# A gated recurrence with a maxout network behind it: the first part reordered around products of constants, block loads split, a third output buffer

## The chip, the cores and the metric

The kernel runs on one core of a Trainium2 chip. The metric is the device time of one execution in microseconds, from launch to end; several runs of the same kernel give a median and a spread. All tensors lie in the chip's memory when the program starts, and the outputs lie there when it ends.

## The reference

The work has two stages. The first is a gated recurrence over 768 time steps, for 4 batches and 8 heads of dimension 48:

```python
f = 1.0 / (1.0 + np.exp(-f_logit))
for t in range(S):                                        # S = 768
    state = f[:, :, t, :, None] * state + einsum('bhd,bhe->bhde', k[:, :, t], v[:, :, t])
    y[:, :, t] = einsum('bhd,bhde->bhe', q[:, :, t], state)
x = y.transpose(0, 2, 1, 3).reshape(B * S, H * D)         # 3072 x 384
h = maximum(maximum(x @ w1, x @ w2), x @ w3)              # 384 -> 768
out = h @ w_out                                           # 768 -> 384
```

The second is a network on its 3072 rows: three products from 384 to 768 columns, their element-wise maximum, and a product back to 384. The four weight matrices arrive as 64-bit floats, everything else as 32-bit floats.

## The kernel before

**Units.** The recurrence is cut into 24 units. A unit holds 64 time steps of 2 batches, so 128 rows. Four units, 512 rows, make a group, and each group goes through the network as one "FFN": FFN 0 for units 0 to 3, up to FFN 5 for units 20 to 23. Within a unit the recurrence is done in its chunked form: running products of the gates from both ends of the chunk, a masked 64x64 product of queries and keys per head and batch, and a state of 48x48 per head that is carried from unit to unit of the same two batches.

**Stages of a unit**, each a function, with the engines in it:

- `load` and `load_v`: the loads of f, k, q and of v, all issued by SyncE (SP). The first eight units load rows, two transfers per tensor (L158). Later units load two at a time as 32x32 blocks, 8 transfers per tensor and so 24 for two units (L173), issued in the pass of each even unit. v always comes by rows into four buffers.
- `sigmoids`: TensorE (PE) transposes f, ScalarE (ACT) takes the sigmoid (L251). For blocks, ACT takes the sigmoid, and VectorE (DVE) does the transposes in `after` and `before` (L238).
- `after`: a DVE scan of the gates (`r`, L273), the reciprocal, and `kh` from k. `before`: the second scan (`prod`, L287) and `qh` from q. The products that make `kh` and `qh` are on DVE for the first eight units and on GpSimd (POOL) later (L280, L291); for these later units q is first turned by DVE into `qt`.
- `carry`: POOL multiplies the old state with the unit's gate product.
- `keys`: PE transposes `kh` (L306), ACT copies the result to `ks` (L308).
- `pairs`: 32 small matrix passes of `kh` with `qh` into `a` (L319), then the mask product `at` on DVE (L322).
- `values`: passes of `at` with v (L333) and of `ks` with v (L342) into `y`, then DVE adds the carried state (L350).
- `finish`: passes of the state with `qh` into `y` (L363), then ACT copies `y` to `heads` (L369).
- `pack`: transfers that move `heads` to `xT`, the layout that the network reads (L380), ten for a whole group. They go out on SP alone, or on SP and ACT by turns.

**The network.** `ffn(g, xT)` is a Python generator. It has 18 input steps, 6 column blocks times w1, w2, w3, each of three 128x512 products (L392). ACT copies the first of three to `top` (L396), DVE takes the maxima of the other two with it, `top` and then `hm` (L398). Four output steps follow, each of six 128x384 products (L411), ACT's copy to `o` (L414) and two output transfers (L418). `fill(n)` takes n steps from the FFNs that are pending, so the order of the program places pieces of one group's network between the stages of the next group's units. PE runs a full-precision 32-bit product as two passes; the records of the trace count passes.

**The weights.** They are brought to 32 bits on the chip in 24 pieces, 18 of the input matrices and 6 of `w_out`. `load_weights` loads a piece into one of 12 `raw` buffers (L199). `round_begin` takes the upper and the lower words: ACT (L211), two short DVE operations (L212, L213), ACT (L216), and a POOL addition (L217). `round_end` has the last DVE operation (L225), which writes `w_in` or `w_out`. Pieces 0 to 2 are done in the first part of the program. The rest is done inside the steps of FFN 0, each `round_begin` one piece ahead of its `round_end`.

**Buffers.** PSUM holds two buffers of the FFN's products `p`, which the transposes of k and q of the first four units use too, two for transposes, one for `a`, one for `y`. Other tiles have two buffers unless said otherwise. The two sets of buffers for f, k, q change from rows to blocks at unit 8; `pad_blocks` then sets six stripes of them, with six POOL memsets each, after units 4 and 6 (L143).

**What sets the order.** The program is written out by hand: each engine runs its instructions in the order in which the Python code issues them, SP and ACT their transfers likewise, and the stages wait for each other through semaphores. A transfer's completion is counted on one of eight semaphores that SP and ACT share, and a transfer waits for the earlier one that used its semaphore. After all else, the kernel looks whether a gate product came out too small: DVE reduces `ends` to `least` (L539), PE sums it over the partitions (L542), the result goes to `low`, every engine reads it (L732), and a second way of doing the whole work is skipped by a branch (L733).

## Time and profile before

| what | value |
|---|---|
| three timed runs | 503.88, 501.72, 504.91 us; median 503.88 |
| the profiled execution: its time | 504.31 us |
| its span, first to last instruction | 502.6 us |
| mean granted TensorE clock | 0.966 |
| PE busy | 467.9 us (93%) |
| DVE busy | 217.2 us (43%) |
| ACT busy | 108.7 us (22%) |
| POOL busy | 98.7 us (20%) |
| chain that ended last | PE 80%, DVE 6%, DMA 4%, SP's queue 4% |

The profile divides the span into 40 slices of 12.6 us; a digit is the busy share in tenths, and the row PEclk has the clock that the throttle granted to PE, also in tenths. A row of the order of time has the start, the duration, the engine, the line, the operation with its output and inputs, and the count of records in the group; in brackets stands the idle time ahead of it and what released it. A row of the stretches has the stretch (from:to in us), its length, then busy time and count of PE, of PE's weight loads, of DVE, ACT and POOL, and in its last three columns the granted clock, the DMA share and the GB/s. A row of a line's transfers to landing has the least, the median and the largest time from issue to landing, of the transfers of one tile in a stretch. "SPq" and "ACTq" are the queues of transfer issues on SP and ACT. The page's row of a line has its busy time and the mean of one in ns.

### The profile page before, as it was taken

The numbers are of one execution on the slowest core, as the hardware profiler recorded it, in microseconds if no ns is written. First come the engines' busy times: TensorE is split into PE (matmuls) and PEld (weight loads), VectorE is DVE, ScalarE is ACT, GpSimd is POOL, SyncE is SP. The second block draws the span as 40 slices with busy tenths as digits, with TensorE's granted clock in tenths as the row PEclk, the third lists the DMA queues.
The fourth block names the chain that finished last, engine by engine and source line by source line (L and its number), as shares of the span: only waits on it lengthen the run. The fifth ranks groups of instructions, "written<-read, shape, count | busy, mean of one in ns | idle before, by whom it ended". The sixth has DMA issues, their size and how long they took to land.

```text
span 502.6 us, 9969 instructions
## 1 busy us (share of the span) xinstructions
PE 467.9 (93%) x4067; PEld 250.9 (50%) x4067; DVE 217.2 (43%) x346; ACT 108.7 (22%) x227; POOL 98.7 (20%) x132
## 2 busy tenths in 40 slices
PE   5755999996989999999999999999999999999994
PEld 4642555543635455645545654545644545544452
DVE  7852787787225435135535226533325620012100
ACT  2340445540212211202220211220220111100000
POOL 2111356564021212021112022112112200000000
PEclk9875999998999999999999999999999999999998
DMA  9995996720156612266602276402460011200011
GB/s 129 199 179 157 268 243 143 93 59 1 40 87 109 88 27 65 46 79 110 85 2 63 56 88 109 66 16 57 78 105 18 1 36 37 55 0 0 1 28 42
DMA packets 170007, 38.51 MB, mean 77 GB/s; under 512 B 154976, under 2 KB 168800, under 8 KB 169952
## 3 DMA queue, kind: packets, MB, share of 16 engines
q1 hardware_dynamic: 166208, 36.50, 41.5%
q10 hardware_dynamic: 3744, 1.28, 1.3%
q8 instruction: 34, 0.56, 0.5%
q14 instruction: 21, 0.17, 0.1%
HBM read 28.31 MB, written 4.72 MB: 66 GB/s over the span
## 4 chain that ended last, share of the span: by engine, by line
PE 80%; DVE 6%; DMA 4%; SPq 4%; ACT 1%; issue 1%; POOL 1%; ACTq 0%; DVEq 0%; POOLq 0%
PE p L392 53%; PE p L411 17%; SPq L158 3%; PE y L363 2%; PE y L333 2%; DMA xT<-heads 2%; PE a L319 2%; PE tr L306 2%; PE y L342 1%; DMA v_ld<-in_v_dram 1%; POOL top_bits L217 1%; PE tr L234 1%; DVE top_bits L213 1%; DMA k_ld<-in_k_dram 1%; DVE top_bits L212 1%
## 5 line engine op out<-in xcount | busy, mean ns | idle before, releaser
L392 PE MATMUL p<-xT,w_in 128*128 128x512 f32 x648 | 291.9, 602 | 7.3 <-DMA xT<-heads 5.1
L392 PEld LDWEIGHTS p<-xT,w_in 128*128 128x128 f32 x648 | 120.5, 191 | 147.0 <-issue 134.1
L411 PE MATMUL p<-w_out,hm 128*128 128x384 f32 x288 | 98.8, 501 | 4.3 <-DVE w_out L225 4.3
L411 PEld LDWEIGHTS p<-w_out,hm 128*128 128x128 f32 x288 | 55.5, 195 | 44.7 <-DVE w_out L225 5.6
L398 DVE TENSOR_TENSOR top<-p,top 128x512 f32<-128x512 f32 x36 | 24.8, 690 | 106.3 <-PE p L392 106.3
L396 ACT COPY top<-p 128x512 f32<-128x512 f32 x36 | 21.1, 586 | 191.5 <-PE p L392 191.5
L279 POOL COPY ends<-r 128x8 f32<-128x8 f32 x24 | 4.6, 193 | 194.2 <-DVE r L273 194.2
L398 DVE TENSOR_TENSOR hm<-p,top 128x512 f32<-128x512 f32 x36 | 24.6, 684 | 38.2 <-PE p L392 38.2
L322 DVE TENSOR_TENSOR at<-a,mask 128x512 f32<-128x512 f32 x24 | 16.5, 689 | 52.8 <-PE a L319 52.8
L217 POOL TENSOR_TENSOR top_bits<-top_bits,rest_bits 128x384 uint32<-128x384 uint32 x24 | 27.2, 1133 | 50.3 <-DVE top_bits L213 27.9
L414 ACT COPY o<-p 128x384 f32<-128x384 f32 x24 | 11.4, 477 | 107.8 <-PE p L411 99.0
L287 DVE TENSOR_TENSOR_SCAN prod<-gate,from_inv 128x520 f32<-128x520 f32 x24 | 32.4, 1349 | 0.0
L273 DVE TENSOR_TENSOR_SCAN r<-gate,from_one 128x520 f32<-128x520 f32 x24 | 30.9, 1288 | 2.9 <-issue 2.2
L369 ACT COPY heads<-y 64x256 f32<-64x256 f32 (+1 forms) x72 | 26.6, 369 | 14.3 <-PE y L363 13.3
L291 POOL TENSOR_TENSOR qh<-qt,prod 128x512 f32<-128x512 f32 x16 | 18.8, 1178 | 41.7 <-DVE qt L238 41.7
L333 PEld LDWEIGHTS y<-at,v_ld 64*64 64x64 f32 x768 | 13.9, 136 | 20.9 <-issue 16.7
L333 PE MATMUL y<-at,v_ld 64*64 64x64 f32 x768 | 17.3, 227 | 5.7 <-ACT rest_bits L216 2.7
L308 ACT COPY ks<-tr 128x512 f32<-128x512 f32 x22 | 12.9, 586 | 41.2 <-PE tr L306 40.9
L280 POOL TENSOR_TENSOR kh<-kt,r 128x512 f32<-128x512 f32 x16 | 19.0, 1186 | 14.2 <-DVE kt L238 14.2
L297 POOL TENSOR_TENSOR state<-st,ends 128x384 f32<-128x384 f32 x22 | 21.1, 958 | 0.2
L238 DVE STREAM_TRANSPOSE gate<-sig 128x512 f32<-128x512 f32 x16 | 11.3, 708 | 21.2 <-ACT sig L254 21.2
L319 PE MATMUL a<-qh,kh 48*64 48x64 f32 x768 | 16.5, 225 | 0.5 <-DVE qh L291 0.5
(64 smaller groups left out, 269.9 us busy)
## 6 DMA issues: line engine op xcount, KB each, us to landing
raw<-in_moe_w_dram SPq DMA_DIRECT2D x18, 384.0 KB, 5.1
v_ld<-in_v_dram SPq DMA_DIRECT2D x48, 96.0 KB, 3.3
out_dram<-o SPq DMA_DIRECT2D x48, 96.0 KB, 2.2
raw<-in_moe_w_out_dram SPq DMA_DIRECT2D x6, 384.0 KB, 4.1
xT<-heads SPq DMA_DIRECT2D x30, 72.0 KB, 2.1
f_ld<-in_f_logit_dram SPq DMA_DIRECT2D x32, 64.0 KB, 2.9
k_ld<-in_k_dram SPq DMA_DIRECT2D x32, 64.0 KB, 2.8
q_ld<-in_q_dram SPq DMA_DIRECT2D x32, 64.0 KB, 2.8
```

Source lines behind the costliest of these rows:

```text
L217: nc.gpsimd.tensor_tensor(top, top, rest, op=ALU.add)
L273: nc.vector.tensor_tensor_scan(r[:, 0:LEN][:, ::-1], flat(gate)[:, ::-1], flat(from_one)[:, ::-1], 1.0, op0=ALU.mult, op1=ALU.max)
L280: (nc.vector if u < BY_ROWS else nc.gpsimd).tensor_tensor(kh.rearrange("p h a t -> p a h t"), kt, by_batch(r[:, 1:LEN + 1].rearrange("p (x ...
L287: nc.vector.tensor_tensor_scan(flat(prod), flat(gate_tiles[u % 2]), flat(from_inv[u % 2]), 1.0, op0=ALU.mult, op1=ALU.max)
L297: nc.gpsimd.tensor_tensor(t, states[u % 2], ends[:, u, :].unsqueeze(2).to_broadcast([128, 2 * HP, D]), op=ALU.mult)
L319: nc.tensor.matmul(p[t, par, hp * C:(hp + 1) * C], lhsT=kh[r, hp, a, :], rhs=qh[r, a, hp, :], start=True, stop=True)
L333: nc.tensor.matmul(y[o:o + DP, a, hp * C:(hp + 1) * C], lhsT=v_ld[s, 2 * hp + par, :], rhs=d["at"][s, par, hp, :], start=(hp == 0), stop=F ...
L369: nc.scalar.copy(heads[o, :, t0 + a * C:t0 + (a + 1) * C], y[i, a, 0:HP * C].rearrange("p (h t) -> p h t", h=HP))
L392: nc.tensor.matmul(p, lhsT=w_in[i][:, kt, j * 128:(j + 1) * 128], rhs=xT[:, kt, :], start=(kt == 0), stop=(kt == NK - 1))
L396: nc.scalar.copy(top, p)
L398: nc.vector.tensor_tensor(hm[:, j, :] if i == 2 else top, p, top, op=ALU.max)
L411: nc.tensor.matmul(p[:, 0:DM], lhsT=hm[:, j, i * UT:(i + 1) * UT], rhs=w_out[:, j, :], start=(j == 0), stop=(j == NJ - 1))
```

## The change

It has seven parts.

1. **Rounding in three parts.** `round_begin` keeps the two ACT operations; the two DVE operations and the POOL addition become `round_middle`. The ACT operations of pieces 0 and 1 stand ahead of `values(2)`; within FFN 0 a piece is begun two ahead of its `round_end` instead of one.
2. **Order of the first loads and of the pack.** f(3) goes ahead of v(1), v(2) ahead of the first three weight pieces. Of unit 4 only f and k are loaded ahead of the pack; q and v are issued behind it.
3. **Products of constants.** `busy(n)` issues n products of the identity with `from_one`, 128x256 each, into a buffer `p` that nothing reads: one each after `pairs(1)`, `pairs(2)` and `pairs(3)`, and 14 behind `finish(3)` and the pack.
4. **Pads.** `pad_blocks` becomes a generator; each step of FFN 0, input or output, takes one memset of it.
5. **Output buffers.** `o` has three buffers instead of two.
6. **Block loads and unit 8.** At an odd unit u, the blocks of f for units u+3 and u+4 are loaded (for u of 5, 9, 13 and 17 those of all three tensors); for u of 7, 11, 15 and 19 k and q follow in the next unit's pass, k ahead of `values`, q behind the next `fill`. At unit 8 the fill ahead of `keys` is left out.
7. **The look at the gate products** stands behind eight fill steps after the last pack, ahead of the other steps of the last FFN, instead of at the end.

```diff
             def pad_blocks(i):
                 for nm, pad in PADS.items():
                     for p0 in (32, 96):
-                        nc.gpsimd.memset(blocks[nm][i][p0:p0 + 32, :, :, D - 32:], pad)
+                        yield nc.gpsimd.memset(blocks[nm][i][p0:p0 + 32, :, :, D - 32:], pad)
...
+            def words(n):
+                w = raw[n].rearrange("p (c two) -> p c two", two=2)
+                return w[:, :, 0], w[:, :, 1]
+
             def round_begin(n):
                 if n in raw:
-                    words = raw[n].rearrange("p (c two) -> p c two", two=2)
-                    lo, hi = words[:, :, 0], words[:, :, 1]
+                    lo, hi = words(n)
                     top = work.tile([128, PIECE], U32, name="top_bits", bufs=4)
                     nc.scalar.activation(top.bitcast(FP32), hi.bitcast(FP32), AF.Abs)
+                    rest = work.tile([128, PIECE], U32, name="rest_bits", bufs=3)
+                    nc.scalar.activation(rest, lo, AF.Copy, scale=2.0 ** -29)
+                    halfway[n] = (top, rest)
+
+            def round_middle(n):
+                if n in raw:
+                    top, rest = halfway[n]
                     nc.vector.tensor_scalar(top.bitcast(FP32), top.bitcast(FP32), HI_MIN, None, op0=ALU.max)
                     nc.vector.tensor_scalar(top, top, 3, 0x3FFFFFF8, op0=ALU.logical_shift_left, op1=ALU.bitwise_and)
-                    rest = work.tile([128, PIECE], U32, name="rest_bits", bufs=3)
-                    nc.scalar.activation(rest, lo, AF.Copy, scale=2.0 ** -29)
                     nc.gpsimd.tensor_tensor(top, top, rest, op=ALU.add)
-                    halfway[n] = (top, hi)
...
                                 round_end(r)
-                                if r + 1 < len(pieces):
-                                    round_begin(r + 1)
+                                if r + 2 < len(pieces):
+                                    round_begin(r + 2)
+                                    round_middle(r + 2)
                             load_weights(2, r + 1)
+                            next(pads, None)
...
-                    o = work.tile([UT, DM], FP32, name="o")
+                    if g == 0:
+                        next(pads, None)
+                    o = work.tile([UT, DM], FP32, name="o", bufs=3)
...
+            def busy(n):
+                p = ps_f.tile([128, TOK], FP32, name="p")
+                for _ in range(n):
+                    nc.tensor.matmul(p[:, 0:256], lhsT=ident, rhs=from_one.rearrange("p x t -> p (x t)")[:, 0:256],
+                                     start=True, stop=True)
+
+            pads = iter(())
...
                 load(2)
+                load(3, one, "f")
                 load_v(1)
-                load(3)
+                load(3, one, "kq")
+                load_v(2)
                 load_weights(3)
-                load_v(2)
                 load_v(3)
...
                     pairs(u + 1)
+                    busy(1)
                     finish(u)
                     before(u + 2)
...
+                for n in range(2):
+                    round_begin(n)
                 values(2)
+                for n in range(2):
+                    round_middle(n)
                 keys(3)
                 finish(2)
                 load_weights(3)
-                load(GRP)
-                load_v(GRP)
-                round_begin(0)
+                load(GRP, one, "fk")
                 pairs(3)
-                round_begin(1)
+                busy(1)
                 round_begin(2)
+                round_middle(2)
                 values(3)
-                for n in range(3):
-                    round_end(n)
-                round_begin(3)
+                round_end(0)
                 nc.tensor.transpose(ps_tr.tile([128, 128], FP32, name="tr"), ident, ident)
                 finish(3)
+                round_end(1)
+                round_end(2)
                 pack(0, GRP - 1, xT, both)
+                for n in range(3, 5):
+                    round_begin(n)
+                    round_middle(n)
+                busy(14)
+                load(GRP, one, "q")
+                load_v(GRP)
                 load_weights(3)
...
-                    fill(2 if u % 2 and u > 2 * GRP else 1)
+                    fill(0 if u == 2 * GRP else 2 if u % 2 and u > 2 * GRP else 1)
...
-                    if u + 2 < NU and (u % 2 == 0 or u + 2 < BY_ROWS):
+                    if u + 2 < BY_ROWS:
                         load(u + 2)
+                    if BY_ROWS <= u + 3 < NU and u % 2:
+                        load(u + 3, one, "fkq" if u % GRP == 1 else "f")
...
                     fill(1)
+                    if BY_ROWS <= u + 2 < NU and u % GRP == 0:
+                        load(u + 2, one, "k")
                     values(u)
                     if n < NU:
                         before(n)
                         carry(n)
                         if n in (5, 7):
-                            pad_blocks(n // 2 % 2)
+                            pads = pad_blocks(n // 2 % 2)
                     fill(1)
+                    if BY_ROWS <= u + 2 < NU and u % GRP == 0:
+                        load(u + 2, one, "q")
...
                 pending.append(ffn(NU // GRP - 1, xT))
+                fill(8)
+
+                least = work.tile([128, 1], FP32, name="least")
+                nc.vector.tensor_reduce(out=least, in_=ends.rearrange("p u a -> p (u a)"), op=ALU.min, axis=AX.X)
+                nc.vector.tensor_scalar(least, least, P_MIN, None, op0=ALU.is_lt)
+                n_low = ps_tr.tile([1, 1], FP32, name="tr")
+                nc.tensor.matmul(n_low, lhsT=least, rhs=ones, start=True, stop=True)
+                nc.vector.tensor_copy(low, n_low)
                 fill(99)
```

The lines removed at the end are the same five that are added above it, without the fill.

How the instructions move shows at three places. In the orders, a number behind a name is its buffer: v_ld_128 to v_ld_131 are the four buffers of v (units 0 to 3, then 4 to 7), f_ld_110 and f_ld_111 the two for f, k_ld_112 and k_ld_113 for k, q_ld_114 and q_ld_115 for q. Lines of the changed kernel are up to 11 higher around the change (L158 becomes L159, L199 L200, L211 L212, L216 L215, L306 L315, L308 L317, L369 L378, L380 L389, L392 L401, L411 L422).

SP's queue from the loads of unit 3 to the first pack, before (v of unit 1, v_ld_129, was issued just ahead):

```order
L158 DMA f_ld_111<-in_f_logit_dram 64x8x48 x2
L158 DMA k_ld_113<-in_k_dram 64x8x48 x2
L158 DMA q_ld_115<-in_q_dram 64x8x48 x2
L199 DMA raw<-in_moe_w_dram 128x3x256 x3
L158 DMA v_ld_130<-in_v_dram 64x8x48 x2
L158 DMA v_ld_131<-in_v_dram 64x8x48 x2
L199 DMA raw<-in_moe_w_dram 128x3x256 x3
L158 DMA f_ld_110<-in_f_logit_dram 64x8x48 x2
L158 DMA k_ld_112<-in_k_dram 64x8x48 x2
L158 DMA q_ld_114<-in_q_dram 64x8x48 x2
L158 DMA v_ld_128<-in_v_dram 64x8x48 x2
L380 DMA xT<-heads 48x512
```

and with the change:

```order
L159 DMA f_ld_111<-in_f_logit_dram 64x8x48 x2
L159 DMA v_ld_129<-in_v_dram 64x8x48 x2
L159 DMA k_ld_113<-in_k_dram 64x8x48 x2
L159 DMA q_ld_115<-in_q_dram 64x8x48 x2
L159 DMA v_ld_130<-in_v_dram 64x8x48 x2
L200 DMA raw<-in_moe_w_dram 128x3x256 x3
L159 DMA v_ld_131<-in_v_dram 64x8x48 x2
L200 DMA raw<-in_moe_w_dram 128x3x256 x3
L159 DMA f_ld_110<-in_f_logit_dram 64x8x48 x2
L159 DMA k_ld_112<-in_k_dram 64x8x48 x2
L389 DMA xT<-heads 48x512
```

The load of v for unit 2 (v_ld_130) stands ahead of the weight pieces now, and the first pack follows k of unit 4 (k_ld_112); q and v of that unit (q_ld_114, v_ld_128) stand behind the pack.

ACT's order from behind the heads of unit 1 to the heads of unit 3, before:

```order
L308 COPY ks<-tr 128x512
L369 COPY heads<-y 128x4x64
L369 COPY heads<-y 64x4x64 x2
L211 ACTIVATE top_bits<-raw 128x384
L216 ACTIVATE rest_bits<-raw 128x384
L211 ACTIVATE top_bits<-raw 128x384
L216 ACTIVATE rest_bits<-raw 128x384
L211 ACTIVATE top_bits<-raw 128x384
L216 ACTIVATE rest_bits<-raw 128x384
L211 ACTIVATE top_bits<-raw 128x384
L216 ACTIVATE rest_bits<-raw 128x384
L369 COPY heads<-y 128x4x64
```

and with the change:

```order
L212 ACTIVATE top_bits<-raw 128x384
L215 ACTIVATE rest_bits<-raw 128x384
L212 ACTIVATE top_bits<-raw 128x384
L215 ACTIVATE rest_bits<-raw 128x384
L317 COPY ks<-tr 128x512
L378 COPY heads<-y 128x4x64
L378 COPY heads<-y 64x4x64 x2
L212 ACTIVATE top_bits<-raw 128x384
L215 ACTIVATE rest_bits<-raw 128x384
L378 COPY heads<-y 128x4x64
```

Two pairs of rounding operations stand ahead of the copy of `ks` for unit 3 (the second `ks` here), one pair behind the heads of unit 2; the fourth pair of before has moved behind the pack.

PE's order from the values of unit 7 to those of unit 8, around the end of FFN 0, before (each row of w_out counts products, six to an output step; the fill steps of FFN 1 begin with the last row):

```order
L333 MATMUL y<-at,v_ld_131 64x64 x16
L342 MATMUL y<-v_ld_131,ks 64x48 x16
L411 MATMUL p<-w_out,hm 128x384 x12
L306 MATMUL tr<-ident,kh 128x128 x4
L363 MATMUL y<-qh,state 48x64 x16
L319 MATMUL a<-qh,kh 64x64 x16
L411 MATMUL p<-w_out,hm 128x384 x12
L333 MATMUL y<-at,v_ld_128 64x64 x16
L342 MATMUL y<-v_ld_128,ks 64x48 x16
L392 MATMUL p<-xT,w_in_63 128x512 x3
```

and with the change:

```order
L342 MATMUL y<-at,v_ld_131 64x64 x16
L351 MATMUL y<-v_ld_131,ks 64x48 x16
L422 MATMUL p<-w_out,hm 128x384 x6
L315 MATMUL tr<-ident,kh 128x128 x4
L372 MATMUL y<-qh,state 48x64 x16
L328 MATMUL a<-qh,kh 64x64 x16
L422 MATMUL p<-w_out,hm 128x384 x12
L342 MATMUL y<-at,v_ld_128 64x64 x16
L351 MATMUL y<-v_ld_128,ks 64x48 x16
L422 MATMUL p<-w_out,hm 128x384 x6
L401 MATMUL p<-xT,w_in_63 128x512 x3
```

One output step instead of two stands between the values of unit 7 and the transposes and `a` products of unit 8, and one more stands behind the values of unit 8.

8 lines of the change are left out of this document (1 added, 7 removed).

## The prediction

> **What bounds the kernel now.** I read the slices of the page first, then PE's order of time, then the waits of the queues in the two stretches where PE stands.
>
> ```profile
> PE   5755999996989999999999999999999999999994
> PEclk9875999998999999999999999999999999999998
> ```
>
> A slice is 12.6 us. From the 13th, so from 151 us, to the last but one each digit of PE is 9 and each of its clock 9: nothing is to be had there; it can only be spoilt. What can be gained lies before that and behind the last matmul. PE's rows of that time, with the wait ahead of each in brackets:
>
> ```profile
> 27.80 1.03 PE L333 MATMUL y<-at,v_ld 64*64 64x64 f32 x30 [2.28 <-DMA v_ld<-in_v_dram]
> 35.10 0.93 PE L333 MATMUL y<-at,v_ld 64*64 64x64 f32 x32 [2.67 <-ACT rest_bits L216]
> 43.29 2.05 PE L392 MATMUL p<-xT,w_in 128*128 128x512 f32 x2 [4.13 <-DMA xT<-heads]
> 119.08 0.91 PE L411 MATMUL p<-w_out,hm 128*128 128x384 f32 x2 [2.86 <-DVE w_out L225]
> 121.47 7.78 PE L411 MATMUL p<-w_out,hm 128*128 128x384 f32 x14 [1.48 <-DVE w_out L225]
> 141.95 3.46 PE L392 MATMUL p<-xT,w_in 128*128 128x512 f32 x7 [2.18 <-ACT o L414]
> 433.14 46.51 PE L392 MATMUL p<-xT,w_in 128*128 128x512 f32 x108
> 46.34 3.75 PE p L392 x4
> 50.09 1.71 PE tr L234 x8
> 51.80 2.97 PE p L392 x6
> ```
>
> The last three are from the chain that ended last. At full clock a pass of 512 columns takes 46.51/108 = 0.43 us; at 46.34 four take 3.75, twice as long. The granted clock (the third column from the right) shows why:
>
> ```profile
> 21.00:22.00 1.00, 1.00 (x55) 0.95 (x47) 0.16 (x1) 0.37 (x1) 0.00 (x0) 0.87 1.02 312
> 25.00:26.00 1.00, 0.52 (x4) 0.28 (x2) 1.00 (x2) 0.00 (x0) 0.00 (x0) 0.92 1.40 137
> 52.00:53.00 1.00, 1.00 (x3) 0.31 (x2) 0.87 (x1) 1.00 (x4) 0.90 (x1) 0.77 1.54 152
> 120.00:121.00 1.00, 0.00 (x0) 0.00 (x0) 0.14 (x1) 0.00 (x0) 0.82 (x1) 0.86 0.00 0
> 127.00:128.00 1.00, 1.00 (x3) 0.55 (x3) 0.00 (x0) 0.00 (x0) 0.00 (x0) 0.72 0.00 0
> ```
>
> With 0.5 and 1.0 as the two values, the clock changes at 21.7, 25.2, 52.5, 120.7 and 127.4: distances of 3.4, 27.3, 68.2 and 6.7, all multiples of 3.41 us. So a window of 3.41 us sets the clock of the next one; after the stall of 2.86 us the clock was half for two windows.
>
> **The first part** (gain 7.9). Today unit 2's values wait at 27.80 for a load, unit 3's at 35.10 for DVE, the first FFN step for the pack into xT.
>
> ```profile
> 19.11 1.69 SPq L199 DMA_DIRECT2D raw<-in_moe_w_dram  x3
> 20.85 2.96 SPq L158 DMA_DIRECT2D v_ld<-in_v_dram  x4
> DMA to landing us min/median/max: 3.9/4.1/4.3
> 24.76 0.69 DVE L322 TENSOR_TENSOR at<-a,mask 128x512 f32<-128x512 f32 x1 [0.40 <-PE a L319]
> 33.07 0.54 ACT L211 ACTIVATE top_bits<-raw 128x384 f32<-128x384 f32 x1
> 39.22 1.14 ACT L369 COPY heads<-y 128x256 f32<-128x256 f32 x3 [2.48 <-PE y L363]
> 29.22 1.58 SPq L158 DMA_DIRECT2D k_ld<-in_k_dram  x2
> DMA to landing us min/median/max: 6.3/6.3/6.4
> 112.29 0.69 PE L333 MATMUL y<-at,v_ld 64*64 64x64 f32 x32 [0.41 <-issue]
> ```
>
> The first landing row is that of the three weight loads, the second that of the k load above it. The load v_ld(2) moves ahead of the weights, to 19.11; what is issued there lands in about 4.1, so near 24, and values(2) then wait for their own mask product (24.76 + 0.69): about 25.3, 2.5 earlier. Then ACT: today L211 starts at 33.07, behind unit 2's heads, and the mask product of unit 3 stands on DVE behind the two DVE operations that need it: values(3) at 35.10 wait for round 0, not for work of their own. Now ACT does rounds 0 and 1 ahead (their weights issue at 20.5 and 21.1 and land by 26; four operations of at most 0.54, to 28.2). From values(2): two groups of 32 matmuls (1.2; one has 0.69 at full clock and they overlap) to 26.5, the transposes (0.5) beside the state add (0.55) and finish(2) to 27.7, pairs(3) to 28.3; DVE meanwhile has four short operations of rounds 0 and 1 (at most 0.56 each, as L225 below), so the mask product runs from 28.5 to 29.2, values(3) to 30.4, the add and finish(3) to 31.6, the heads (1.14) to 32.8 instead of 40.36. Rows in which PE is at half clock or DVE meets POOL would make it 34.5.
>
> The pack does not follow at that distance. Its transfers now stand in SP's queue right behind k(4): its second transfer issues near 29.9 (two take 1.58 from 29.22) and lands only at 36.2, and by the program's waits SP's fourth issue of the pack waits for that landing. The last issue comes near 37, and with some 2.4 for its flight (less than the 2.9 that today pass from the heads' end to PE's start) xT is whole at 39.4; q(4) and v(4) behind it are needed only two steps later.
>
> The 14 dummy matmuls are 28 passes of 256 columns: 6.0 us at full clock, 12 at half. From 31.6 to 33.6, with one or two half-clock windows, they end between 39.3 and 42.2. I take 40.7 for the first FFN pass, at full clock. Today's equal: at 52.5 six passes (2.6), eight transposes (0.9, half of the 1.71 above) and 0.4 of a later one were done, as if PE had begun at 48.6 at full clock. Gain 48.6 - 40.7 = **7.9**. Ends: 9.2, and 3 if all 28 run at half clock (begin 45.6). The three single dummies cost nothing: each stands where PE next waits for DVE or a load; without that cover, 0.4 to 0.9 each.
>
> The Trainium skill ("TensorE: Matmul & The Clock Gate", Part 1: The HAM clock gate) gives a free-running window of 3.4 us, half clock after a whole idle one, full clock after 3.4 us of sustained work. The window agrees with the rows. The rest does not: after 46.34 PE took 6.2 us of work to reach full clock, and at 120.7 it fell though two matmuls stood in that window. By the page the dummies would end near 39 and the clock term below would be nothing: 3 us less in all.
>
> **The end of FFN 0** (gain 9.6).
>
> ```profile
> 105.67 1.09 POOL L143 MEMSET f_ld<- 32x512 f32 x2
> 109.34 0.99 POOL L217 TENSOR_TENSOR top_bits<-top_bits,rest_bits 128x384 uint32<-128x384 uint32 x1
> 110.37 0.56 DVE L225 SCALAR_TENSOR_TENSOR w_out<-raw,top_bits 128x384 uint32<-128x384 uint32 x1 [2.14 <-DMA xT<-heads]
> ```
>
> Six memsets stood ahead of a POOL addition that DVE waited 2.14 us for (the named DMA had long nothing to do with it). Spread over six steps they hold one addition by 0.55 (half of 1.09), and rounds begin two steps ahead, so DVE does not wait. The w_out stalls go: 2.86 + 1.48 = **4.3**; with them the two half-clock windows, 120.7 to 127.4, less 0.6 idle: half of 6.1, **3.1**. If DVE stays late, 2 us of this remain. The third buffer of o removes the wait at 141.95, **2.2**: out-transfers no longer stand behind all of the pack.
>
> **A new wait at unit 8** (cost 3.7). Today two out-steps (7.8 us) stand between values(7) and pairs(8); the fill of 0 leaves one, 12 passes of 0.32 (384/512 of 0.43) = 3.9. pairs(8) needs qh(8):
>
> ```profile
> 112.11 0.68 DVE L398 TENSOR_TENSOR top<-p,top 128x512 f32<-128x512 f32 x1
> 114.64 1.58 DVE L273 TENSOR_TENSOR_SCAN r<-gate,from_one 128x520 f32<-128x520 f32 x1
> 117.27 0.65 DVE L398 TENSOR_TENSOR hm<-p,top 128x512 f32<-128x512 f32 x1
> 121.80 1.23 DVE L287 TENSOR_TENSOR_SCAN prod<-gate,from_inv 128x520 f32<-128x520 f32 x1
> 122.95 0.68 DVE L238 STREAM_TRANSPOSE qt<-q_ld 128x512 f32<-128x512 f32 x1
> 123.71 1.17 POOL L291 TENSOR_TENSOR qh<-qt,prod 128x512 f32<-128x512 f32 x1 [2.89 <-DVE qt L238]
> ```
>
> Let X be PE's end of step 17. From step 16's maximum DVE has 112.11 to 117.27, 5.2 us, until step 17's, and PE only 2.6 for a step: the latter starts at X + 2.6 even if DVE is not late. It, two w_out (0.56 each), the state add (0.55, of the same 384 columns), scan, qt and POOL's product: 0.65 + 1.1 + 0.55 + 1.2 + 0.7 + 1.2 brings X + 8.0. PE: values 1.1, out-step 3.9, keys and finish 1.0: X + 6.0. So PE stands **2.3** (1.7 to 2.9; the whole unit's later work is queued behind it). A window that is half idle may lose the clock: 2 in 3 for a window or two, 1.7 each, I put **1.4** (0 to 3.4).
>
> **The end of the program** (cost 0.5).
>
> ```profile
> L539 DVE TENSOR_REDUCE least<-ends 128x1 f32<-128x192 f32 x1 | 0.3, 311 | 0.0
> L733 PEldq COMPARE_BRANCH x1: 4318/4318/4318, 496.1 to 496.1; - x1
> L733 SPq COMPARE_BRANCH x1: 45/45/45, 498.0 to 498.0; - x1
> ```
>
> The matmul on least now stands in PE's queue behind step 4 of the last FFN; DVE must first take that step's maximum (0.68), the reduction (0.31) and a comparison of one column (0 to 0.31): PE, with all later steps behind it, waits 1.0 to 1.3, I take **1.3**. In return SP's load of low leaves the tail, between the two branches above; of these 1.9 us part is the last output's flight, which stays: 0 to 1.9, I take **0.8**.
>
> The split of the block loads I cost at nothing.
>
> ```profile
> 87.52 4.29 SPq L173 DMA_DIRECT2D f_ld<-in_f_logit_dram  x8
> ```
>
> Eight issues take 4.29, 0.54 each. k(10) is issued behind the third out-copy and needed 16 us of PE work later, for these 4.3 and a landing near 3, by the rows above at most 6.3; v(7), now behind 24 block issues (13 us), lands 10 us ahead of its use.
>
> **The sum.** -7.9 - 4.3 - 3.1 - 2.2 + 2.3 + 1.4 + 1.3 - 0.8 = -13.3. The profiled execution had a span of 502.6 and a time of 504.3; it becomes 489.3 and 491.0. The median shown, 503.88, is 0.4 under that execution: **490.6**. All good ends give 17 less than today, all bad ones 3.
>
> **The rivals.**
> - *Cold dummies* (0.17): the gate stays at half clock through all 28 passes, as it did for 9 us after 43.29; begin at 45, 4.3 later: 494.9. Against it: PE is then busy without a gap, as after 46.34.
> - *No wait at unit 8* (0.14): DVE is less late than I count and the clock holds: 3.7 less, 486.9. Against it stand the 5.2 us between the two maxima.
> - *DVE as the bound of FFN 0* (0.10): rounds and units fill DVE nearly to the PE work there, and the earlier start only ends in the same w_out stall and its clock: 7.4 more, 498.0.
> - *A blocked SP* (0.04): in before SP stood 21.7 us within one pack, since a transfer shares its completion semaphore with one that ACT issues later:
>
> ```profile
> SPq L380 <- DMA xT<-heads: 21.7, 1, 21.7
> ```
>
> If such a block falls on a split k load, it passes the 9 us that this load has to spare by 13, and PE stands for these and about 2 of clock: one such block gives 505.6, slower than now. By the program's waits k and q wait for SP's own loads, which speaks against it.
>
> **How the numbers follow.** The forecast has 0.55, with 486 to 495 of its own. To leave out 2 in 10, the range takes in the unit 8 rival and the cold dummies, and most of the third: 485.0 to 497.5. A measurement of this kernel can tell about 1% (499 to 509 is no change). Faster: forecast, the first two rivals and a third of the third, 0.89; the rest of the third, 0.07, is no change; slower 0.04.
>
> **What would show it.** Right: values(2) near 25 and the heads of unit 3 done by 35; dummies at half clock first, first w_in pass at 39 to 42.5 and full clock from then; no wait at L422 for w_out above 0.5; a wait of about 2 at pairs(8) for POOL; about 1.3 ahead of the matmul on least. Wrong: raw weights landing after 28, so that unit 3's ks copy is late; a wait of PE in 150 to 400; SP waiting over 9 us ahead of a block load.

## The result, and the profile after

The changed kernel takes 489.68 us, the median of 4 runs (486.72 to 491.43), against 503.75 for the kernel before (4 runs). The ratio is 0.9719, with a 95% interval of 0.9662 to 0.9776. The forecast was 490.6. The profiled execution has a time of 489.50, a span of 487.8 (502.6 before) and a mean granted clock of 0.990 (0.966 before).

The same two rows of the page's slices, of the changed kernel; a slice is 12.2 us here:

```profile
PE   5779999998999999999999999999999999989994
PEclk9979999999999999999999999999999999999998
```

From the fourth slice on PE shows 9 nearly everywhere. Of the dips of before in the slices 10 and 12 (6 and 8) one 8 is left. To see what came from where, one cuts the span at work that both programs do in the same order. PE's order of time has such points. Of the kernel before, two that were not shown yet (the first FFN step that runs 12 passes in a row, and the last products of all):

```profile
55.04 5.32 PE L392 MATMUL p<-xT,w_in 128*128 128x512 f32 x12
479.49 15.64 PE L411 MATMUL p<-w_out,hm 128*128 128x384 f32 x48
```

And of the changed kernel, the rows that answer to those of the prediction (L342 is L333 of before, L401 is L392, L422 is L411, L448 the products of constants):

```profile
25.02 0.98 PE L342 MATMUL y<-at,v_ld 64*64 64x64 f32 x30 [0.96 <-DMA v_ld<-in_v_dram]
30.44 1.25 PE L342 MATMUL y<-at,v_ld 64*64 64x64 f32 x30 [1.43 <-ACT heads L378]
34.39 7.84 PE L448 MATMUL p<-from_one,ident 128*128 128x256 f32 x28
42.08 2.74 PE L401 MATMUL p<-xT,w_in 128*128 128x512 f32 x6
48.54 5.32 PE L401 MATMUL p<-xT,w_in 128*128 128x512 f32 x12
103.67 0.69 PE L342 MATMUL y<-at,v_ld 64*64 64x64 f32 x32
108.14 1.56 PE L422 MATMUL p<-w_out,hm 128*128 128x384 f32 x4 [0.55 <-DVE w_out L234]
112.15 0.69 PE L328 MATMUL a<-qh,kh 48*64 48x64 f32 x32 [1.42 <-POOL qh L300]
125.77 7.89 PE L401 MATMUL p<-xT,w_in 128*128 128x512 f32 x18
147.60 2.84 PE L401 MATMUL p<-xT,w_in 128*128 128x512 f32 x6 [0.68 <-ACT top L405]
431.94 0.19 PE L581 MATMUL tr<-ones,least 128*1 128x1 f32 x2 [1.30 <-DVE least L579]
465.64 15.64 PE L422 MATMUL p<-w_out,hm 128*128 128x384 f32 x48
```

| stretch | before | after | gained | forecast |
|---|---|---|---|---|
| start to the step with 12 passes in a row | 55.04 | 48.54 | 6.5 | 7.9 |
| from there to the values of unit 7 | 57.25 | 55.13 | 2.1 | 0 |
| from there to FFN 1's first product | 29.66 | 22.10 | 7.6 | 5.9 |
| from there to the end of the last product | 353.18 | 355.51 | -2.3 | -1.3 |
| the rest of the span | 7.5 | 6.5 | 0.9 | 0.8 |
| sum | 502.6 | 487.8 | 14.8 | 13.3 |

In the third stretch the brackets make the sum: the waits for w_out went from 2.86 + 1.48 to 0.55, the wait of 2.18 at FFN 1's first step went, the 6.7 us at half clock (3.05 us of work) went, and 1.42 for POOL's `qh` came: 3.8 + 2.2 + 3.05 - 1.4 = 7.6. In the fourth there are the 1.30 at the matmul on `least`, as forecast, and 0.68 that nobody had forecast. So the size is right, and so are most of the terms. The experiments ask whether the parts of the change that the prediction named are what brought them.

### The profile page after: what moved, and what is told of

Its sections match the earlier page's. It is cut to its first block, busy times and chain, and to the rows that moved or that the text cites. A ratio compares the mean times of both kernels' runs of the same rounds, so it can differ in the third digit from the quotient of the medians.

```text
span 487.8 us, 10037 instructions
## 1 busy us (share of the span) xinstructions
PE 466.6 (96%) x4101; PEld 252.5 (52%) x4101; DVE 223.2 (46%) x346; ACT 109.4 (22%) x227; POOL 99.5 (20%) x132
## 4 chain that ended last, share of the span: by engine, by line
PE 87%; SPq 5%; DMA 3%; DVE 1%; ACT 1%; issue 1%; POOL 0%; ACTq 0%; DVEq 0%; POOLq 0%
PE p L401 55%; PE p L422 19%; SPq L159 3%; PE y L342 3%; PE y L372 2%; PE a L328 2%; PE y L351 2%; PE p L448 2%; PE tr L315 1%; SPq L174 1%; DMA raw<-in_moe_w_dram 1%; PE tr L243 1%; DMA k_ld<-in_k_dram 1%; SPq L389 1%; DMA v_ld<-in_v_dram 1%
## 5 line engine op out<-in xcount | busy, mean ns | idle before, releaser
L401 PE MATMUL p<-xT,w_in 128*128 128x512 f32 x648 | 288.1, 596 | 0.7 <-ACT top L405 0.7
L401 PEld LDWEIGHTS p<-xT,w_in 128*128 128x128 f32 x648 | 120.0, 190 | 138.4 <-issue 132.0
L422 PE MATMUL p<-w_out,hm 128*128 128x384 f32 x288 | 96.6, 490 | 0.5 <-DVE w_out L234 0.5
L422 PEld LDWEIGHTS p<-w_out,hm 128*128 128x128 f32 x288 | 53.8, 190 | 38.1 <-issue 2.4
L227 POOL TENSOR_TENSOR top_bits<-top_bits,rest_bits 128x384 uint32<-128x384 uint32 x24 | 28.3, 1178 | 40.2 <-DVE top_bits L225 25.5
L296 DVE TENSOR_TENSOR_SCAN prod<-gate,from_inv 128x520 f32<-128x520 f32 x24 | 34.7, 1448 | 0.0
L378 ACT COPY heads<-y 64x256 f32<-64x256 f32 (+1 forms) x72 | 26.6, 369 | 9.5 <-PE y L372 8.3
L342 PEld LDWEIGHTS y<-at,v_ld 64*64 64x64 f32 x768 | 14.4, 137 | 18.1 <-issue 15.0
L317 ACT COPY ks<-tr 128x512 f32<-128x512 f32 x22 | 12.9, 585 | 39.3 <-PE tr L315 39.0
L306 POOL TENSOR_TENSOR state<-st,ends 128x384 f32<-128x384 f32 x22 | 20.4, 925 | 0.2
L342 PE MATMUL y<-at,v_ld 64*64 64x64 f32 x768 | 18.0, 228 | 2.5 <-ACT heads L378 1.4
L224 DVE TENSOR_SCALAR top_bits<-top_bits 128x384 f32<-128x384 f32 x24 | 12.6, 525 | 9.9 <-ACT top_bits L212 9.9
```

What stands on the lines that cost most here:

```text
L227: nc.gpsimd.tensor_tensor(top, top, rest, op=ALU.add)
L296: nc.vector.tensor_tensor_scan(flat(prod), flat(gate_tiles[u % 2]), flat(from_inv[u % 2]), 1.0, op0=ALU.mult, op1=ALU.max)
L306: nc.gpsimd.tensor_tensor(t, states[u % 2], ends[:, u, :].unsqueeze(2).to_broadcast([128, 2 * HP, D]), op=ALU.mult)
L342: nc.tensor.matmul(y[o:o + DP, a, hp * C:(hp + 1) * C], lhsT=v_ld[s, 2 * hp + par, :], rhs=d["at"][s, par, hp, :], start=(hp == 0), stop=F ...
L378: nc.scalar.copy(heads[o, :, t0 + a * C:t0 + (a + 1) * C], y[i, a, 0:HP * C].rearrange("p (h t) -> p h t", h=HP))
L401: nc.tensor.matmul(p, lhsT=w_in[i][:, kt, j * 128:(j + 1) * 128], rhs=xT[:, kt, :], start=(kt == 0), stop=(kt == NK - 1))
```

## The experiments

In all of them the times are medians of 4 to 10 runs, beside runs of the kernel before on the same chip. Since single executions of the changed kernel lie up to 4.7 us apart, the points of the table above say more than the times: the start of the step with 12 passes (48.54 after, 55.04 before) for the first part, and the distance from the values of unit 7 to FFN 1 (22.10 and 29.66) for the end of FFN 0. The first of these has a spread of its own. Six of the kernels below have the first part of the change (two_o, unsplit, unit8_fill, pads_bulk, one_ahead, look_split), and in the one profiled execution of each that step starts at 47.32 to 49.92, and `finish(3)`, the last work ahead of the products of constants, at 32.00 to 34.49. So a difference of 1 us at this point, between two single executions, can be chance.

### The products of constants

They were taken out of the change, and put alone into the kernel before.

no_dummies, made from the change:

```diff
-                busy(14)
```

> The change without its 14 products of constants behind the pack; the three single ones stay. Theory: xT is whole near 42.0 us with or without them, because SP's fourth pack transfer waits for k of unit 4, so the first FFN product still starts at 42; what they buy is the clock alone. PE idles from 34.4 to 42, two whole windows of 3.41 us, and stays at half clock for two to three windows from 42 on: 3.1 to 4.6 us more, 492.8 to 494.3. Rival: the products themselves hold PE up and the pack would be there at 40 or before: the first product starts at 40 or before and the time is 487.5 to 489.7.

dummies_alone, made from the kernel before, with the function `busy` of the change added:

```diff
                 pack(0, GRP - 1, xT, both)
+                busy(14)
```

> The kernel before with the 14 products of constants behind the first pack and nothing else changed. Theory: they run from 39.2, at half clock to about 45.5, and end near 48.3, while xT is whole at 46.3; the FFN starts 2 us later but at full clock, against today's start that equals 48.6 at full clock: gain 0.3, 503.6. Rival: the products are the main part of the change's gain, by the clock that they win: 3 us or more, 500.9 or less. If the clock does not rise while they run, they end at 51.2 and it is 2.6 slower.

Without them the change takes 489.25 us (486.94 to 490.67), ratio 0.9706 (0.9658 to 0.9753): no difference from the change with them. Alone they make the kernel before slower: 506.06 (504.01 to 507.35) against 503.33, ratio 1.0051 (1.0022 to 1.0079). My expectation fell both times. Of the first kernel the rival's numbers came out, of the second neither's. PE's order of time without them:

```profile
38.00 5.94 PE L401 MATMUL p<-xT,w_in 128*128 128x512 f32 x6 [5.01 <-DMA xT<-heads]
48.04 5.32 PE L401 MATMUL p<-xT,w_in 128*128 128x512 f32 x12
```

and two of the stretches, with the granted clock third from the right:

```profile
42.00:44.00 2.00, 2.00 (x5) 0.82 (x4) 0.00 (x0) 0.02 (x1) 0.00 (x0) 0.50 0.86 148
44.00:46.00 2.00, 2.00 (x11) 1.52 (x10) 0.73 (x3) 1.96 (x4) 0.04 (x1) 0.86 1.05 372
```

I had taken xT to be needed whole. But each product waits only for the parts of xT that it reads: the first step starts at 38.00, 4 us before the change's, while SP's pack transfers are still being issued until 38.6. It runs at half clock until 44.6 and is at the step with 12 passes at 48.04, against 48.54 in the change. `finish(3)` began 1.03 us earlier in that execution (32.33 against 33.36), so from there on the products are worth 0.5 us: the full clock from 42.08 on, less 4 us in which PE could have worked at half. Counted from `finish(3)`, the step comes 15.7 us later without them and 14.9 to 15.4 later in the seven executions with them, so they are worth 0.3 to 0.8. Alone in the kernel before they are worth 2.0 at that point (53.05 against 55.04), since there the half clock lasted until 52.5. This is lost again at the end of FFN 0, where the wait for `o` doubles:

```profile
53.05 5.32 PE L392 MATMUL p<-xT,w_in 128*128 128x512 f32 x12
141.41 11.97 PE L392 MATMUL p<-xT,w_in 128*128 128x512 f32 x24 [4.44 <-ACT o L414]
```

FFN 1 starts at 141.41 against 141.95: of the 2.0 us won 90 us earlier 0.5 are left, and the half-clock window that follows (the row at 141.41 takes 11.97 us for its 24 passes, 10.76 before) takes these too. The next group of experiments shows what that wait hangs on.

### The wait ahead of FFN 1

The forecast gave 2.2 us to the third buffer of `o`. Four kernels look at it: the change with two buffers of `o`; the change with whole block loads; the split alone in the kernel before; and the change with the fill of one ahead of unit 8 put back.

two_o, made from the change:

```diff
-                    o = work.tile([UT, DM], FP32, name="o", bufs=3)
+                    o = work.tile([UT, DM], FP32, name="o")
```

> The change with two buffers of o instead of three. Theory: the out-transfers of FFN 0 still stand behind pack transfers on SP, so ACT's last copy to o waits and PE's first or second step of FFN 1 with it: 2.2 us more, 491.9. Rival: with one output step moved behind the values of unit 8 the copies lie far enough apart and the third buffer is not needed: no wait, 489.7.

unsplit, made from the change (split_alone is the reverse, in the kernel before):

```diff
-                    if u + 2 < BY_ROWS:
+                    if u + 2 < NU and (u % 2 == 0 or u + 2 < BY_ROWS):
                         load(u + 2)
-                    if BY_ROWS <= u + 3 < NU and u % 2:
-                        load(u + 3, one, "fkq" if u % GRP == 1 else "f")
...
-                    if BY_ROWS <= u + 2 < NU and u % GRP == 0:
-                        load(u + 2, one, "k")
...
-                    if BY_ROWS <= u + 2 < NU and u % GRP == 0:
-                        load(u + 2, one, "q")
```

> The change with the block loads issued whole again, all 24 transfers in the pass of each even unit, as before; the rest of the change stays. The forecast costed the split at nothing. Theory now: it is the split that removed the wait at FFN 1's first step. By the program's waits, with whole block loads the second transfer of the pack of units 4 to 6 shares its completion count with a transfer that ACT issues only behind the heads of unit 7; SP stands until about 114, and out-transfers and the pack of unit 7 come later: SP waits 10 us or more within that pack, and PE 2 to 4 us ahead of FFN 1: 491.7 to 493.7. Rival (the forecast): the split is worth nothing, the third buffer of o carried this term: 489.7.

> The kernel before with the block loads split around the groups as in the change, and nothing else. Theory: SP no longer stands 21.7 us within the pack of units 4 to 6, so ACT's copy to o does not wait and PE's wait of 2.18 us at FFN 1's first step goes; the waits for w_out (2.86 and 1.48) and their clock stay: 501.0 to 502.0. Rival: the wait moves to another transfer on the same count, or the wait at FFN 1 comes from the two buffers of o: 503.3 to 504.

unit8_fill, made from the change:

```diff
-                    fill(0 if u == 2 * GRP else 2 if u % 2 and u > 2 * GRP else 1)
+                    fill(2 if u % 2 and u > 2 * GRP else 1)
```

> The change with the fill of one ahead of the stages of unit 8 put back (fill 0 becomes fill 1). Theory: two output steps stand again between the values of unit 7 and the a products of unit 8, 3.9 us more PE work, so the wait of 1.42 us for POOL's qh goes and nothing takes its place, since the third buffer of o is enough; the wait of 0.68 us near 147, which comes from which p buffer a step was given, may go too: 487.5 to 488.3. Rival: the fill of 0 is needed so that an output step stands behind the values of unit 8; without it the first step of FFN 1 waits for the pack of unit 7 or for o, 2 us or more: 490 or above.

With two buffers the change takes 489.96 us (488.20 to 492.32), ratio 0.9735 (0.9682 to 0.9787), and FFN 1's first product follows the output step ahead of it without any wait:

```profile
123.06 4.14 PE L422 MATMUL p<-w_out,hm 128*128 128x384 f32 x12
127.04 7.89 PE L401 MATMUL p<-xT,w_in 128*128 128x512 f32 x18
```

In the change, with the loads split, the third buffer is not needed; the rival held.

The split alone takes 501.60 (501.01 to 502.31) against 503.01, ratio 0.9974 (0.9963 to 0.9985). In its trace the stalls for w_out stand as before (2.88 and 1.48), and only the wait ahead of FFN 1 is gone, 139.65 instead of 141.95. The reason is on SP's queue. Of the kernel before, of the split alone, and of the change, the ten transfers of the pack of units 4 to 6:

```profile
107.20 27.89 SPq L380 DMA_DIRECT2D xT<-heads  x10
```

```profile
107.13 6.28 SPq L380 DMA_DIRECT2D xT<-heads  x10
139.65 5.63 PE L392 MATMUL p<-xT,w_in 128*128 128x512 f32 x12
```

```profile
99.61 6.28 SPq L389 DMA_DIRECT2D xT<-heads  x10
```

27.89 us became 6.28. In the kernel before, one of these transfers counts on the same semaphore as a transfer that ACT issues behind the heads of unit 7, and SP stood until that had landed; out-transfers and the next pack stood behind it. With the loads split, the transfers fall differently on the eight semaphores. So the part of the change that the forecast costed "at nothing" is, in the kernel before, worth the whole 2.3 us at this place; the median of the time fell by 1.4.

In the change it is not needed, though. With whole block loads it takes 490.20 (489.76 to 491.42), ratio 0.9754 (0.9732 to 0.9777). SP stands again,

```profile
SPq L389 <- DMA xT<-heads: 15.6, 1, 15.6
```

but PE waits only 0.23 us ahead of FFN 1, not the 2 to 4 that I expected. Two parts of the change that are left can cover it: the output step that now stands behind the values of unit 8, and the third buffer, which here is in use. Of this kernel, ACT's fourth copy to `o` and SP's output transfers of the second to the fourth:

```profile
125.53 0.48 ACT L427 COPY o<-p 128x384 f32<-128x384 f32 x1 [4.67 <-PE p L422]
141.14 4.04 SPq L431 DMA_DIRECT2D out_dram<-o  x6
```

With two buffers the fourth copy would take the buffer of the second, whose transfers were issued only from 141.14 on, and by that order it would have to wait 16 us or more (an estimate from these two rows). A kernel with whole loads and two buffers was not run, so the share of each cover is not shown. With the output step put back to its old place and the loads split, a wait comes back in another form:

```profile
122.81 1.12 PE L401 MATMUL p<-xT,w_in 128*128 128x512 f32 x2
125.78 9.68 PE L401 MATMUL p<-xT,w_in 128*128 128x512 f32 x22 [1.85 <-issue]
```

Here the 1.42 for `qh` and the 0.68 near 147 are gone, as the theory had it, and 1.85 has come ahead of the second product of FFN 1, near the 2 us of the rival; it ends about 3 us after SP's last pack transfer for that xT was issued (122.7). The time is 488.19 (487.67 to 488.99), ratio 0.9705 (0.9667 to 0.9743), not to be told from the change. So the wait ahead of FFN 1 has more than one cover. In the kernel before, the free SP queue alone removes it, with two buffers. In the change the moved output step and the third buffer together leave 0.23 of it without the free queue, and the free queue and the third buffer leave a wait of 1.85 without the moved step. The third buffer is not needed once the loads are split and the step is moved; alone in the kernel before it was not run.

### The stalls for w_out

pads_bulk, made from the change:

```diff
-                            pads = pad_blocks(n // 2 % 2)
+                            for _ in pad_blocks(n // 2 % 2):
+                                pass
```

> The change with the six pad memsets issued together again, behind units 4 and 6, as before. Theory: a piece is begun two steps ahead now, which gives POOL's addition more slack than the 3.3 us that the six memsets take, so DVE waits under 1 us and PE's wait for w_out stays near 0.5: 489.5 to 490.5. Rival: the memsets were the cause of the stalls for w_out: PE waits 2 us or more there again and loses the clock for one or two windows: 492.5 to 495.

one_ahead, made from the change:

```diff
-                                if r + 2 < len(pieces):
-                                    round_begin(r + 2)
-                                    round_middle(r + 2)
+                                if r + 1 < len(pieces) and r > 3:
+                                    round_begin(r + 1)
+                                    round_middle(r + 1)
```

> The change with pieces begun one ahead of their last operation again within FFN 0 (from piece 5 on); pads stay spread. Theory: DVE then waits for POOL's addition between the middle and the end of a piece, 1 us or more in several of the last steps, and with DVE as full as it is there (5.2 us between two maxima) PE waits for w_out 2 us or more and may lose the clock: 492 to 495. Rival: the memsets alone had caused the stall and one ahead is enough: 489.5 to 490.5.

PE's waits of the two kernels in that place:

```profile
108.02 1.56 PE L422 MATMUL p<-w_out,hm 128*128 128x384 f32 x4 [0.81 <-DVE w_out L234]
```

```profile
108.52 0.91 PE L422 MATMUL p<-w_out,hm 128*128 128x384 f32 x2 [0.64 <-DVE w_out L234]
110.91 0.91 PE L422 MATMUL p<-w_out,hm 128*128 128x384 f32 x2 [1.48 <-DVE w_out L234]
114.45 0.69 PE L328 MATMUL a<-qh,kh 48*64 48x64 f32 x32 [1.59 <-POOL qh L300]
```

In one_ahead DVE waits 1.17 us for POOL's addition at two of the last pieces; the second wait is the one ahead of PE's 1.48:

```profile
110.30 0.56 DVE L234 SCALAR_TENSOR_TENSOR w_out<-raw,top_bits 128x384 uint32<-128x384 uint32 x1 [1.17 <-POOL top_bits L227]
```

With the memsets together the wait grows from 0.55 to 0.81 and the time stays, 489.58 (488.59 to 492.81), ratio 0.9751 (0.9709 to 0.9793). With one piece ahead, the waits are 0.64 + 1.48, the wait for `qh` is 1.59, a half-clock window follows, and the time is 493.51 (491.11 to 493.53), ratio 0.9796 (0.9766 to 0.9826). Both theories held: with pieces begun two ahead only 0.55 of the stalls is left with the pads spread and 0.81 with them together, so spreading them is worth 0.3 us there. But with one ahead and the pads spread, 2.12 us of stalls are left and not the 4.34 of before: the 1.48 is there unchanged, and the 2.86 has become 0.64. That part went with the spread pads or with the rounding in three parts, which one_ahead has too; one ahead with the pads together was not run. The distance from the step with 12 passes to the values of unit 7 is 55.13 with bulk pads and 55.54 with one ahead, 57.25 in the kernel before. So of the 2.1 us that the table has there, 0.4 are from the second piece ahead and nothing from the pads; the rest (the split of `round_begin`, so that DVE no longer meets ACT's first operation, is the candidate) was not taken apart.

### The order of the first part

rounds_behind, made from the change:

```diff
-                for n in range(2):
-                    round_begin(n)
                 values(2)
-                for n in range(2):
-                    round_middle(n)
...
                 load(GRP, one, "fk")
+                round_begin(0)
+                round_middle(0)
                 pairs(3)
                 busy(1)
-                round_begin(2)
-                round_middle(2)
+                for n in (1, 2):
+                    round_begin(n)
+                    round_middle(n)
```

> The change with the rounding of pieces 0 to 2 put back behind the heads of unit 2 on ACT, as before; first loads, products of constants and everything later stay. The measure is the start of the FFN step with 12 passes in a row, 48.5 in the change and 55.0 in the kernel before. Theory: in the change ACT's copy of ks for unit 3 and the heads of unit 2 stood behind the second piece, whose load landed only at 27.8, so the two orders cost nearly the same: the mask product of unit 3 moves from 29.5 to about 30.4, the step to 48.5 to 49.5, the time 489.5 to 491. Rival: taking ACT's rounding out of the way is what removed the wait of 2.67 us ahead of the values of unit 3: that wait returns, the step comes at 51 or later, 492 or above.

v2_behind, made from the change:

```diff
-                load_v(2)
                 load_weights(3)
+                load_v(2)
```

> The change with v of unit 2 loaded behind the first three weight pieces again; the rest stays. Theory: the values of unit 2 wait for that load as before, from 25.0 to 27 or later, and all that follows them on PE, DVE and ACT up to the pack comes as much later: the step with 12 passes at 50 to 51, 491 to 492. Rival: the weight pieces, now issued 1.3 us earlier, let ACT's rounding start earlier, and the pack waits for k of unit 4 anyway: the step at 48.5, 489.7.

PE's order of time with the rounding behind the heads of unit 2, and with v of unit 2 behind the weights:

```profile
30.91 0.69 PE L342 MATMUL y<-at,v_ld 64*64 64x64 f32 x32 [2.15 <-DVE at L331]
49.35 5.32 PE L401 MATMUL p<-xT,w_in 128*128 128x512 f32 x12
```

```profile
27.55 1.06 PE L342 MATMUL y<-at,v_ld 64*64 64x64 f32 x30 [2.99 <-DMA v_ld<-in_v_dram]
36.91 6.31 PE L448 MATMUL p<-from_one,ident 128*128 128x256 f32 x28
49.52 5.32 PE L401 MATMUL p<-xT,w_in 128*128 128x512 f32 x12
```

The step with 12 passes comes at 49.35, 0.8 later, with the rounding put back: my theory for that point (48.5 to 49.5), not the rival's 51, although a wait of 2.15 stands ahead of the values of unit 3 (1.43 in the change, 2.67 before). The time is 491.89 (490.76 to 492.55), ratio 0.9757 (0.9730 to 0.9784), above the 491 that I gave it. 1.7 us of the difference arise at 113.8, where that execution fell to half clock for one window (the last section tells of this), so the time is not evidence for the rival; the other three executions have no trace.

With v of unit 2 behind the weights its values wait until 27.55, 2.5 later, and `finish(3)` begins 2.95 later, but the step with 12 passes comes only 1.0 later, at 49.52, a little less than I expected, since PE was at full clock by then and the 28 passes took 6.31 us instead of 7.84. The time, expected at 491 to 492, is 492.59 (490.44 to 494.19), ratio 0.9784 (0.9753 to 0.9816).

So each of the two moves the step by 1 us or less, and both steps still lie within the 47.32 to 49.92 of the kernels that have the first part of the change. Clear of that spread is only that without the earlier load of v the values of unit 2 come 2.2 us or more later (24.20 to 25.29 in all other kernels with that load order) and `finish(3)` 1.8 or more. What the two are worth together, and the load of f and the three single products, was not tried: most of the first part's gain is shown as a sum only, as the 4.7 us by which `finish(3)` begins earlier (33.36 against 38.05; 3.6 to 6.1 by the spread).

### A version that might beat both

look_split, made from the change:

```diff
+                least = work.tile([128, 1], FP32, name="least")
+                nc.vector.tensor_reduce(out=least, in_=ends.rearrange("p u a -> p (u a)"), op=ALU.min, axis=AX.X)
+                nc.vector.tensor_scalar(least, least, P_MIN, None, op0=ALU.is_lt)
                 fill(8)
-
-                least = work.tile([128, 1], FP32, name="least")
-                nc.vector.tensor_reduce(out=least, in_=ends.rearrange("p u a -> p (u a)"), op=ALU.min, axis=AX.X)
-                nc.vector.tensor_scalar(least, least, P_MIN, None, op0=ALU.is_lt)
                 n_low = ps_tr.tile([1, 1], FP32, name="tr")
```

> The change with the look at the gate products cut in two: DVE's reduction and comparison are issued ahead of the eight fill steps, the matmul on least stays where it is. Theory: PE's wait of 1.30 us at that matmul is DVE's maximum, reduction and comparison behind the step's products; with least long done nothing is waited for: 1.3 us less, 488.4, and no wait in the profile at that matmul. Rival: the matmul waits for its PSUM buffer, not for least, and the wait stays: 489.7.

best, made from look_split:

```diff
-                load(GRP, one, "fk")
...
-                busy(14)
-                load(GRP, one, "q")
+                busy(11)
+                load(GRP)
                 load_v(GRP)
```

> The change with three edits: the look cut in two, f and k of unit 4 loaded behind the first pack too, and 11 products of constants instead of 14. Theory: SP's fourth pack transfer no longer waits for k of unit 4, the last one is issued near 38 instead of 39.4 and xT is whole at 40.7, where 22 passes end too: first FFN product at 40.7 instead of 42.1, and 1.3 for the look: 2.7 less than the change, 487.0. Rival: f and k of unit 4, now issued near 39, land after 43.5, where PE wants them between FFN steps, and what the pack wins is lost there: 488.4 to 489.5.

With the look cut in two PE's order of time has no wait at that matmul any more, and none of the later ones took its place:

```profile
433.65 0.19 PE L581 MATMUL tr<-ones,least 128*1 128x1 f32 x2
```

The time is 487.02 (484.69 to 491.15), ratio 0.9648 (0.9607 to 0.9689); the profiled execution is the slowest of the four, with 3.54 us for a late load of v ahead of the values of unit 3. The last version:

```profile
34.59 3.23 SPq L389 DMA_DIRECT2D xT<-heads  x5
40.00 2.74 PE L401 MATMUL p<-xT,w_in 128*128 128x512 f32 x6
43.35 0.63 PE L243 MATMUL tr<-ident,k_ld 128*128 128x128 f32 x4 [0.17 <-DMA k_ld<-in_k_dram]
46.83 5.32 PE L401 MATMUL p<-xT,w_in 128*128 128x512 f32 x12
```

The five pack transfers on SP now go out in 3.23 us, without the pause that makes it 4.77 us in the change (35.31 to 40.08). That pause is not for k of unit 4, as the forecast and my expectations had it. Of the change, the last three of SP's five transfers, SP's wait within that pack, and the time to landing of the two transfers of k, which were issued at 30.8 and 31.4:

```profile
38.23 1.85 SPq L389 DMA_DIRECT2D xT<-heads  x3
SPq L389 <- DMA xT<-heads: 1.6, 1, 1.6
DMA to landing us min/median/max: 4.8/4.9/5.1
```

k had landed by 36.2, and SP's third transfer went at 38.23, behind 1.6 us that the profile puts to another transfer of the pack. It is the first of ACT's, issued at 35.70 and landed at 38.17, which counts on the same semaphore: the block of 21.7 us of the kernel before, on a smaller scale. Without f and k ahead of it the pack falls differently on the eight semaphores, and SP does not stand.

The first product starts at 40.00, the step with 12 passes at 46.83, and k of unit 4 is late by 0.17 us; 0.57 more are lost at 68.62 to a load of f. The span is 485.5, 2.3 less than the change's, where 2.7 were expected. The time is 487.48 (486.92 to 488.25, 5 runs), ratio 0.9674 (0.9652 to 0.9695). Against the kernel before that is clear. Against the change (0.9719, 0.9662 to 0.9776) the intervals overlap, and the two were not timed on one chip: the waits removed are shown, a faster median is likely and not shown.

## Why the prediction was right, and which of its steps were not

**The first part** (7.9 forecast, 6.5 measured). Values of unit 2 at 25.02 held (forecast 25.3). The pack did not wait for k of unit 4: SP's fourth transfer went at 38.79, 2.6 us after k had landed, and what held it was ACT's transfer ahead of the third. The heads of unit 3 were done at 35.7, not 32.8. The view of the weight pieces issued between 15 and 25 us, and ACT's order of time, both of the change, tell why:

```profile
DMA to landing us min/median/max: 5.4/6.6/7.2
```

```profile
27.86 0.57 ACT L212 ACTIVATE top_bits<-raw 128x384 f32<-128x384 f32 x1 [0.59 <-DMA raw<-in_moe_w_dram]
28.77 0.58 ACT L317 COPY ks<-tr 128x512 f32<-128x512 f32 x1
34.53 1.14 ACT L378 COPY heads<-y 128x256 f32<-128x256 f32 x3 [3.11 <-PE y L372]
```

The pieces took 5.4 to 7.2 us to land, not the 3.9 to 4.3 of the row that the forecast used. ACT's second piece started at 27.86 only, with `ks` of unit 3 and the heads of unit 2 behind it, and PE lost its clock at 30.7. The 28 passes ended the wait at 42.08, within the forecast's 39.3 to 42.2. The step that failed is the role of these passes: "as if PE had begun at 48.6" was compared with a start of theirs at 40.7, and what PE could do without them was not worked out. Without them it starts at 38.0 on the parts of xT that are there, and ends up 0.5 us behind. They hardly contribute.

The 6.5 is one execution; in the six other kernels with this first part the gain at that step is 5.1 to 7.7. Two small sums of the forecast were off too: from 33.6 with two half-clock windows (6.0 + 3.4) the passes end at 43.0 and not 42.2, and all good ends add to 18 and not 17.

**The end of FFN 0** (9.6 forecast, 9.0 measured, without the wait at unit 8). The w_out stalls and their clock came out as priced: 3.8 of 4.3, and 3.05 of 3.1. Of the two causes named, the pieces begun two ahead are enough without the spread pads; what the pads do without these stays open. The 2.2 us were right, by luck as to the cause: "The third buffer of o removes the wait" is not what happens in the change, since two_o has no wait either. The split of the loads frees SP's queue, and that alone removes the wait in the kernel before. The forecast had costed the split at nothing after having seen SP's block of 21.7 us and only asked where else it might fall. (The clock rose at 127.6 rather than 127.4, since the row 127:128 has 0.72; that moves the term by less than 0.1.)

**Unit 8** (3.7 forecast). The wait was 1.42 instead of 2.3, for the reason given (`qh` from POOL behind a late DVE): POOL's product ended at X + 8.4 (forecast 8.0), and PE stood from X + 7.0 (forecast 6.0), 0.55 of that for `w_out`. The clock held in the profiled execution; over nine executions with this wait it fell in four, 1.7 us each (the last section), which is 0.8 on average where 1.4 was put.

**The end of the program.** PE's 1.30 at the matmul on `least` is the forecast's 1.3, and 0.9 of tail its 0.8.

**What was not forecast.** The gain of 2.1 inside FFN 0: the prediction has no term for that stretch. And the 0.68 at 147.60: by the program's waits, that step of FFN 1 was given the p buffer of the step just before it, so it waits for ACT's copy of it. In unit8_fill, where the steps lie differently, it isn't there. What was missed or priced too low on the good side (2.1 inside FFN 0, 2.3 at unit 8) and what was priced too high or missed on the bad side (1.4 in the first part, 0.6 at the stalls, 0.7 at 147.60, 0.3 in smaller pieces behind it) partly cancel, so the sum (13.3, and 14.8 measured) is nearer than several of its terms; that nearness is luck.

## What to carry to other kernels

Before an engine is kept busy to win its clock, work out what it could do in that time with the parts of its input that have already arrived: half speed early can equal full speed late. A wait that hangs on another queue, here one that stands for another engine's transfer, swallows what is won ahead of it, so look for such a queue first; an edit that only reorders transfers can free it. And when one edit of several removes a wait, take each out by itself, and then in pairs: here the wait had more than one cover, the buffer that the forecast credited was not needed beside the others, and taking out one at a time does not say what it would do without them.

## What the runs showed of the hardware

The clock's windows explain 1.7 us of the spread between executions; the first part, with its 2.6 us, is another source. In nine kernels with the same 1.4 us wait at unit 8, the distance from the values of unit 7 to FFN 1 is 22.1 to 22.5 us in five and 23.8 in four, and the difference of 1.7 is one window of 3.41 us at half clock. The changes of clock in each first part give the window's phase in that execution. The wait began 0.8 to 1.3 us after the start of its window in the four where the clock fell (no_dummies, two_o, rounds_behind, look_split), and 1.5 to 1.9 us after it in the five where it did not (the change, unsplit, pads_bulk, v2_behind, best). Here is the change, then no_dummies, with the idle time near the same place:

```profile
111.00:112.00 1.00, 0.00 (x0) 0.00 (x0) 0.00 (x0) 0.90 (x3) 1.00 (x1) 1.00 0.29 25
113.00:114.00 1.00, 1.00 (x4) 0.60 (x4) 0.61 (x1) 0.00 (x0) 0.95 (x2) 1.00 0.13 33
```

```profile
111.00:112.00 1.00, 0.34 (x21) 0.34 (x24) 0.00 (x0) 0.42 (x2) 1.00 (x2) 1.00 0.60 79
113.00:114.00 1.00, 1.00 (x3) 0.47 (x2) 0.11 (x1) 0.00 (x0) 0.52 (x1) 0.50 0.05 10
```

Why the two groups differ, with as much idle time in both, is open, and the place within the window cannot be the whole rule. In the first part, waits that began 1.6 to 2.0 us after the start of their window, with 1.3 to 1.7 us of idle time within it, took the clock in all five kernels that had one: the change, unsplit, pads_bulk, one_ahead and best. In the change it is the wait of 1.43 ahead of the values of unit 3, from 29.01 to 30.44, in the window from 27.29 to 30.70. The work in the rest of the window differs between the two places, and no run separates it. The way up is plainer: in no_dummies the window from 37.7 to 41.2 has a quarter of a microsecond idle at its start and the clock stays at half; the next, without a gap, is followed by full clock at 44.6. The Trainium skill ("TensorE: Matmul & The Clock Gate", Part 1: The HAM clock gate) asks for 3.4 us of sustained work for full clock. The prediction said that the rows did not agree; counted in fixed windows they do. The other half of that rule, that the clock falls after a wholly idle window, does not hold here: 1.4 us idle in a window were enough four times of nine.
